# Phi products of two groups in one PSUM bank, and slot sums two at a time

## The chip, the cores and the metric

One core of a Trainium2 chip runs the whole program. The metric is the time of the program on the device in microseconds, the median of several runs. Engines are named as in the profile: PE is TensorE (matmuls), PEld its weight loads, DVE is VectorE, ACT is ScalarE, POOL is GpSimd, SP is SyncE, which sends off the DMAs here.

## The reference, cut to what matters

```python
X = rfft(x, axis=1)                       # x: 8 batches x 2496 x 256
Yr = Xr @ w_r - Xi @ w_i + b_r            # and Yi likewise
Yr = sign(Yr) * max(abs(Yr) - 0.01, 0)    # soft threshold, Yi likewise
y = irfft(Y, n=2496)                      # 19968 tokens of 256
logits = y @ phi                          # 32 slots: 8 experts x 4
d = softmax(logits, axis=0)               # over all tokens
slot_input = d.T @ y                      # 32 x 256
slot_out = relu(slot_input @ w1) @ w2     # per expert
out = softmax(logits, axis=1) @ slot_out
```

## The kernel before

The inverse transform is linear, so the kernel never needs y itself: it multiplies the thresholded spectrum by phi (the **Phi product**), transforms the 32 columns of the result back to logits, and sums the slots on the spectrum's side too.

A batch is done in five **groups** (0 to 4) of four frequency rows; eight batches make 40 **steps**, s = 5b + group. A step runs on PE through `px` (second half of the forward transform, two halves c), `pk` and `py` (the linear layer, `lin_k` and `lin_y`, for two halves e of the 256 features, with c 0 and c 1 summed in turn) and, from `lin_y`, on DVE and POOL to the thresholded spectrum `rt`. Between these stand `pa` matmuls, the first half of the forward transform of a later batch.

`tp_p(s)` takes the spectrum `rt` of a step: 8 matmuls of 32 x 128 onto four strips of a bank `pq` (the Phi product), a copy of 128 x 128 by ACT into `lg`, one transposition of `lg` back into the bank, and a signed copy by DVE into `p_sb`. `tp_t` transposes `rt` itself (`pt`) and copies it to tiles `T` for the slot sums.

When all five groups of a batch are in `p_sb`, `c_stages(b)` runs beside the next batch's five steps: `pg`, a DMA through DRAM (`gd`, `gp`), ACT's `chpL` and DVE's `clpL` (a split into two parts), `pL` (logits), DVE's running maxima `mx`, a transposition `pm`, the batch maximum `mall`, `dg`, `pb`, exponentials `ee`, `pe`, a DMA through DRAM again (`ed`, `eb`), `chpd` and `clpd`, `pd`, and `dd`. Then `slots_acc` adds a group's **slot sum** into the bank `pr`: 4 matmuls of 32 x 256 onto its four strips, one call for each of the five groups; group 0's has 4 more of one column (`zcol`). The trace counts two instructions for each of these matmuls, so a Phi product is x16 and a slot sum x8 there. So a slot sum belongs to a batch two before the one whose Phi product stands beside it.

The order of the instructions is written by hand: every piece of work is a generator that yields the time at which its next part stands in the program, a heap calls the parts in order of these times, and each engine keeps that order. A step is four units of that time. `tp_p(s)` stands at 4s + 6.5 (`LAG` is 6), which is between the two c halves of `py` (e = 1) of the step after. `PLAN["pr"]` holds the times of a batch's five slot sums, in units from 20b + 26; before, each stands directly ahead of a Phi product, except batch 4's first, which stands by itself. Tiles come from rings: the banks `px` and `pa`, `pk` and `py`, `pq` and `pt` have two each, `pr` one; `rt` has a ring of four.

Of the kernel before, what the change touches and what calls it, by code (L numbers as in the profile page):

```python
# [11 lines left out]
F32 = mybir.dt.float32  # L12
# [5 lines left out]
B, N, D = 8, 2496, 256  # L18
# [5 lines left out]
S = 32  # L24
# [28 lines left out]
def _constants():  # L53
# [83 lines left out]
    "pe": [11.35, 12.35],  # L137
    "cm": 14.3,
    "pd": [16.75, 17.5],
    "pr": [20.49, 24.49, 28.49, 32.489999999999995, 36.489999999999995],  # L140
    "au": [[1.4, 3.4, 5.4, 7.4, 9.4, 11.4, 13.4, 15.4, 17.4, 19.4],
           [1.4, 3.4, 5.4, 7.4, 9.4, 10.85, 11.7, 13.4, 15.4, 17.4, 18.85, 19.7]],
    "tho": 1.4,
# [5 lines left out]
    "ao": 0.25,  # L149
    "ko": 0.915,  # L150
    "to": 0.7,
    "late": {'6': {'cms': [11.5, 19.69, 854.1, 854.2, 854.2, 854.2], 'pd': [20.25, 20.62], 'pr': [31.55, 31.6, 31.65, 31.7, 31.75], 'pL': [6.05, 6.5], 'pm': 8.05, 'pb': 9.05, 'eo': 0.4, 'pe': [11.1, 11.5], 'pg': [0.875, 1.275], 'fr': {'sinv': 0, 'm2': 0, 'f1': 0, 'suni': 0}}, '5': {'cms': [14.3, 14.8, 15.6, 20.0, 20.8, 21.5], 'pg': [1.1, 1.8], 'pL': [6.1, 6.8], 'pm': 8.05, 'pb': 9.05, 'fr': {'sinv': 1, 'm2': 1, 'f1': 1, 'suni': 0}, 'pe': [11.35, 12.35], 'pd': [18.9, 19.3], 'pr': [40.2, 40.21, 40.22, 40.23, 40.24]}, '4': {'pr': [18.4, 20.49, 24.49, 28.49, 32.49]}},
    "T_": {'wl': [[-45, 'r'], [-44, 'r'], [-43, 'r'], [-31.0, 't'], [-30.7, 't'], [-29.4, 't'], [-27.6, 't'], [-27.8, 't'], [-11, 'a'], [-10.3, 'a'], [-9.6, 'a'], [-9.45, 'sm'], [-9.4, 'xs'], [-8.3, 'x'], [-8.1, 'x'], [1.06, 'x'], [1.07, 'h'], [1.08, 'h'], [13.55, 'h'], [13.55, 'h'], [13.55, 'h'], [13.55, 'h'], [13.55, 'h'], [13.61, 't'], [13.61, 't'], [13.61, 't'], [13.61, 't'], [13.61, 't'], [13.7, 'T'], [13.7, 'T'], [13.7, 'T']], 'cl': 1.02, 'cp': 46.5, 'ct': 46.6, 'du': [[-4.5, 0], [-2.4, 0], [1.2, 0]], 'd1': [5, 2, 4, 0, 0, 0], 'cm': [19.9, 19.91, 19.92, 25, 25.1, 25.2], 'cm7': [0.1, 0.12, 0.3, 0.4, 1, 1], 'ye': 0.2, 'te': [[5.6, 0.2], [5.5, 0.4]], 'pg': [-7, -3.25, -0.35], 'yt': 0.5, 'wr': -30.6, 'tp': [0, 0.9, 1.05, 0.3], 'tt': [[-3.6, -0.3, -0.25, -0.2, -6.5], [0.6, 0.7, 0, 0, 0], [12, 12.1, 12.2, 12.3, 12.4]], 'tg': {(5, 4): ('ps', 'pl'), (5, 0): ('pl', 'ps')}, 'eg': {(5, 4, 1): 'A', (6, 2, 1): 'A', (6, 4, 0): 'V', (6, 4, 1): 'A'}, 'z': 13.55, 'th': [0.1, 0.12], 'tl': [0.2, 0.25]},
    "f1": [1.5, 2.15],
    "ap1": 1.9,
# [30 lines left out]
def fourier_soft_moe_kernel(ctx: ExitStack, tc: tile.TileContext, t: dict, out: bass.AP):  # L186
# [55 lines left out]
    def mm(**kw):  # L242
        tc.keep_in_program_order(nc.tensor.matmul(**kw))  # L243
# [60 lines left out]
    for z, (n, w) in zip((pk0, pk1), PACK.items()):  # L304
        o = 0
# [243 lines left out]
    def lin_y(s, e):  # L549
        b, grp = steps[s]  # L550
        end = s == ns - 1
        t0 = 4 * s + 1 + (PLAN["T_"]["ye"] if end else 1.35) * e
        yield t0
        py = psum("pl", f"py{b}_{grp}_{e}")
        lin(py, e, 0, xts[(s, 0)], grp == 0)
        if s == 0 and e == 0:
            yield t0 + 0.03
        if e == 1 and not end:
            t0 = 4 * s + 3
            yield t0  # L560
# [13 lines left out]
        if b == B - 3 and grp < KG:
            rt = hd_part(f"rt{b}_", grp, e).rearrange("p (j c q) -> p j c q", j=KG, c=2)
        else:
            rt = wtile([128, KG, 2, 64], F32, "T" if b >= B - 2 else "rt", f"rt{b}_{grp}_{e}")
        yield t0 + (PLAN["T_"]["th"][e] if end else PLAN["tho"])
        L_("th", s, e).tensor_scalar(out=rt, in0=ut, scalar1=LAM, scalar2=-LAM, op0=ALU.min, op1=ALU.max)
        yield t0 + (PLAN["T_"]["tl"][e] if end else PLAN['tlo'])  # L580
        L_("tl", s, e).tensor_tensor(out=rt, in0=ut, in1=rt, op=ALU.subtract)
        tts[(s, e)] = rt

    def tp_p(s):
        b, grp = steps[s]
        n = 4 * s + LAG
        d = PLAN["T_"]["tp"] if s >= ns - 2 else PLAN["tp"]
        yield n + d[0]
        if grp == 0:
            psb[b] = wtile([128, K1, S], F32, "p_sb", f"p_sb{b}")  # L590
        pq = psum("pt", f"pq{b}_{grp}")
        ks = slice(grp * KG, grp * KG + KG)
        rv = [tts[(s, e)].rearrange("p j c q -> p j (c q)") for e in range(2)]
        if s == ns - 1:
            for e in range(2):
                for j in range(KG):
                    mm(
                        out=pq[:, 128 + S * j : 128 + S * j + S],
                        lhsT=rv[e][:, j],
                        rhs=phr[:, e, :],  # L600
                        start=(e == 0 and j == 0),
                        stop=(e == 1),
                        skip_group_check=True,
                    )
        else:
            for e in range(2):
                for j in range(KG):
                    mm(
                        out=pq[S * j : S * j + S, 0:128],
                        lhsT=phr[:, e, :],  # L610
                        rhs=rv[e][:, j],
                        start=(e == 0),
                        stop=(e == 1),
                        skip_group_check=True,
                    )
            yield n + d[1]
            lg = wtile([128, 128], F32, "lg", f"lg{b}_{grp}")
            A.copy(out=lg, in_=pq[:, 0:128])
            yield n + d[2]
            tr(pq[:, 128:256], lg, ident)  # L620
        yield n + d[3]
        V.tensor_tensor(
            out=psb[b][:, ks, :],
            in0=pq[:, 128:256].rearrange("p (j s) -> p j s", s=S),
            in1=sgn[:, ks].unsqueeze(2).broadcast_to([128, KG, S]),
            op=ALU.mult,
        )

    def tr(out, in_, identity):
        tc.keep_in_program_order(nc.tensor.transpose(out=out, in_=in_, identity=identity))  # L630
# [544 lines left out]
    rhs = []  # L1175
# [178 lines left out]
```

## Time and profile before

| | us |
|---|---|
| median of 3 runs | 529.37 (529.04 to 529.81) |
| span of the profiled execution | 528.2 |
| PE busy | 508.5 (96%) |
| DVE busy | 410.7 (78%) |
| ACT busy | 311.1 (59%) |
| POOL busy | 295.0 (56%) |

The granted clock of TensorE is at its full level (2.4 GHz) up to the last of forty slices. Busy time of PE counts overlapping matmuls as one; the chain of waits follows the work that ended last backwards, and its entry for an instruction is the time that passed until the next entry, so a run of matmuls reads shorter there than the sum of their own durations. A timeline row that stands for several instructions has the start of the first. In it an idle time stands in brackets with what ended it.

### The profile page before, as it was taken

How to read it: one execution, taken by the hardware profiler on the slowest of the kernel's cores; microseconds unless marked ns; L12 is line 12 of the kernel's file. 1: busy time of each engine (PE TensorE's matmuls, PEld its weight loads, DVE VectorE, ACT ScalarE, POOL GpSimd, SP SyncE). 2: the span in 40 equal slices, each digit the busy share in tenths (PEclk: the TensorE clock that was granted, in tenths of full speed). 3: DMA queues.
4: the chain of work that ended last, by engine and by line, in shares of the span. 5: the costliest groups of instructions: out<-in, count | busy, mean ns of one | idle time of the engine just before them, and what ended most of it. 6: DMA issues, size and time to landing. Idle time of an engine off the chain costs nothing.

```text
span 528.2 us, 12045 instructions
## 1 busy us (share of the span) xinstructions
PE 508.5 (96%) x4473; PEld 442.1 (84%) x4473; DVE 410.7 (78%) x802; ACT 311.1 (59%) x679; POOL 295.0 (56%) x279
## 2 busy tenths in 40 slices
PE   8999999999999999999999999999999999999991
PEld 8888899998898989898989898888998887458880
DVE  3876886799978998899789989887898856256671
ACT  2666666768666866686668665645434346138771
POOL 0567587768675766676667666856575403053310
PEclk9999999999999999999999999999999999999996
DMA  8545456674765565556655665686665477979998
GB/s 296 185 165 186 159 182 224 169 236 125 269 171 177 153 224 157 194 157 217 172 182 149 228 185 199 161 302 181 234 166 158 159 173 210 403 245 397 402 407 338
DMA packets 90002, 114.85 MB, mean 217 GB/s; under 512 B 46462, under 2 KB 65852, under 8 KB 89944
## 3 DMA queue, kind: packets, MB, share of 16 engines
q1 hardware_dynamic: 89233, 112.90, 65.3%
q10 hardware_dynamic: 711, 1.19, 0.7%
q8 instruction: 35, 0.57, 0.4%
q14 instruction: 23, 0.19, 0.1%
HBM read 66.72 MB, written 47.34 MB: 216 GB/s over the span
## 4 chain that ended last, share of the span: by engine, by line
PE 78%; DVE 9%; DMA 4%; ACT 3%; issue 2%; POOL 1%; SPq 1%; ACTq 0%; DVEq 0%; POOLq 0%
PE py L243 19%; PE px L243 12%; PE pq L243 9%; PE pa L243 8%; PE pk L243 8%; PE pt L630 6%; PE pr L243 4%; PE pc L1153 2%; PE pe L243 2%; PE pg L243 2%; PE pL L243 1%; PE po L243 1%; DVE ut L182 1%; PE hps L243 1%; DVE xtl L182 1%
## 5 line engine op out<-in xcount | busy, mean ns | idle before, releaser
L182 POOL TENSOR_TENSOR rt<-ut,rt 128x512 f32<-128x512 f32 x79 | 108.0, 1366 | 21.6 <-DVE rt L182 20.7
L182 POOL TENSOR_TENSOR xs<-xsm,xs 128x256 fp32r<-128x256 f32 x78 | 58.5, 750 | 101.5 <-DVE xs L182 74.1
L182 POOL TENSOR_TENSOR xl<-xr,xh 117x512 fp32r<-117x512 f32 x72 | 99.1, 1377 | 11.5 <-ACT xh L182 11.5
L243 PEld LDWEIGHTS px<-smov,ap 128*128 128x128 f32 x640 | 79.7, 191 | 9.4 <-issue 3.1
L243 PE MATMUL px<-smov,ap 128*128 128x128 f32 x640 | 85.6, 277 | 2.0 <-ACT ast L182 0.8
L182 ACT CAST xth<-px 128x512 fp32r<-128x512 f32 x80 | 47.0, 588 | 55.8 <-PE py L243 33.9
L182 DVE SCALAR_TENSOR_TENSOR ut<-py,pk,k 128x256 f32<-128x256 f32 x160 | 69.5, 476 | 10.7 <-PE py L243 10.2
L182 ACT COPY ast<-pa 128x512 f32<-128x512 f32 x75 | 44.3, 591 | 46.7 <-PE pa L243 46.6
L182 DVE TENSOR_TENSOR xtl<-px,xth 128x512 fp32r<-128x512 f32 x80 | 54.6, 683 | 16.3 <-ACT xsm L182 15.8
L243 PE MATMUL pk<-xs,w_rh 128*128 128x256 f32 (+1 forms) x320 | 66.0, 290 | 0.3 <-POOL xs L182 0.3
L182 DVE TENSOR_SCALAR rt<-ut 128x512 f32<-128x512 f32 x69 | 56.9, 824 | 0.5
L243 PE MATMUL py<-xth,nwsh 128*128 128x256 f32 (+1 forms) x160 | 53.3, 333 | 0.4 <-DVE ut L182 0.2
L243 PEld LDWEIGHTS pk<-xs,w_rh 128*128 128x128 f32 x320 | 51.8, 189 | 1.1 <-POOL xs L182 0.5
L182 ACT CAST xh<-xr 117x512 fp32r<-117x512 f32 x75 | 47.3, 634 | 0.0
L630 PE MATMUL pt<-pk,rt 128*128 128x128 f32 x320 | 45.4, 274 | 0.2
L182 ACT COPY T<-pt 128x512 f32<-128x512 f32 x67 | 39.7, 600 | 8.9 <-PE pt L630 7.5
L243 PE MATMUL py<-xth,wdh 128*128 128x256 f32 (+1 forms) x160 | 44.8, 280 | 0.0
L243 PE MATMUL py<-xtl,nwsh 128*128 128x256 f32 (+1 forms) x160 | 44.5, 278 | 0.0
L243 PE MATMUL py<-xtl,wdh 128*128 128x256 f32 (+1 forms) x160 | 44.5, 278 | 0.0
L243 PE MATMUL py<-xth,wdl 128*128 128x256 f32 (+1 forms) x160 | 44.4, 278 | 0.0
L243 PE MATMUL py<-xth,nwsl 128*128 128x256 f32 (+1 forms) x160 | 44.4, 278 | 0.0
L243 PE MATMUL pk<-xs,w_rl 128*128 128x256 f32 (+1 forms) x160 | 44.4, 277 | 0.0
(195 smaller groups left out, 1200.7 us busy)
## 6 DMA issues: line engine op xcount, KB each, us to landing
out<-ost SPq DMA_DIRECT2D x37, 512.0 KB
xr<-in_x SPq DMA_DIRECT2D x35, 512.0 KB
ap<-adr SPq DMA_DIRECT2D x70, 256.0 KB
adr<-ast SPq DMA_DIRECT2D x21, 768.0 KB
w<-in_moe_w SPq DMA_DIRECT2D x25, 512.0 KB
w<-in_moe_w SPq DMA_DIRECT2D x12, 256.0 KB
x<-in_x SPq DMA_DIRECT2D x11, 256.0 KB
eb<-ed SPq DMA_DIRECT2D x16, 160.0 KB
```

What stands on the lines that cost most here:

```text
L182: return lambda *a, **k: self.tc.keep_in_program_order(f(*a, **k))
L243: tc.keep_in_program_order(nc.tensor.matmul(**kw))
L630: tc.keep_in_program_order(nc.tensor.transpose(out=out, in_=in_, identity=identity))
L1153: nc.tensor.transpose(out=pc[:, i * P1 : (i + 1) * P1], in_=chls[b][x][:, 2 * (r + i) : 2 * (r + i) + 2].rearrange("p g h s -> p (g h s)") ...
```

## The change

Steps in `PAIRED` (groups 1 and 3 of the batches 0 to 6 without step 1, and group 1 of the last batch; 14 steps) no longer have a `tp_p` of their own. The `tp_p` of the step behind takes both: 16 matmuls into 256 columns of one bank, one copy of 128 x 256, two transpositions, one signed copy of 128 x 256. The slot sums of groups 1 and 3 move to the places of groups 0 and 2; of batch 4 the first two stand at the place of group 0 and the other three at that of group 2. Up to batch 4 the `rt` of the first step of a pair lies in a tile `rtx` in a room that batch 0 used and then left, two such tiles in turn, instead of in the ring of four. No matmul is added or taken away, and the transpositions `pt` stay where they were.

```diff
@@ -37,6 +37,7 @@
 XTRA = {2: (2, 5), 3: (5, 8)}
+PAIRED = {NGRP * b + g for b in range(B - 1) for g in (1, 3)} - {1} | {NGRP * (B - 1) + 1}
 
 
 def _tokens():
@@ -137,7 +138,7 @@
     "pd": [16.75, 17.5],
-    "pr": [20.49, 24.49, 28.49, 32.489999999999995, 36.489999999999995],
+    "pr": [20.49, 20.495, 28.49, 28.495, 36.49],
@@ -149,7 +150,7 @@
-    ... '4': {'pr': [18.4, 20.49, 24.49, 28.49, 32.49]}},
+    ... '4': {'pr': [20.49, 20.495, 28.49, 28.495, 28.497]}},
@@ -573,6 +574,10 @@
             )
         if b == B - 3 and grp < KG:
             rt = hd_part(f"rt{b}_", grp, e).rearrange("p (j c q) -> p j c q", j=KG, c=2)
+        elif s in PAIRED and b < B - 3:
+            if e == 0:
+                rtx[s] = hd_tile((len(rtx) + 1) % 2, f"rtx{s}")
+            rt = rtx[s][:, 512 * e : 512 * e + 512].rearrange("p (j c q) -> p j c q", j=KG, c=2)
         else:
             rt = wtile([128, KG, 2, 64], F32, "T" if b >= B - 2 else "rt", f"rt{b}_{grp}_{e}")
         yield t0 + (PLAN["T_"]["th"][e] if end else PLAN["tho"])
@@ -581,17 +586,20 @@
         L_("tl", s, e).tensor_tensor(out=rt, in0=ut, in1=rt, op=ALU.subtract)
         tts[(s, e)] = rt
 
-    def tp_p(s):
+    def tp_p(*group):
+        s = group[-1]
         b, grp = steps[s]
         n = 4 * s + LAG
+        m = len(group)
         d = PLAN["T_"]["tp"] if s >= ns - 2 else PLAN["tp"]
         yield n + d[0]
         if grp == 0:
             psb[b] = wtile([128, K1, S], F32, "p_sb", f"p_sb{b}")
         pq = psum("pt", f"pq{b}_{grp}")
-        ks = slice(grp * KG, grp * KG + KG)
-        rv = [tts[(s, e)].rearrange("p j c q -> p j (c q)") for e in range(2)]
+        ks = slice((grp - m + 1) * KG, grp * KG + KG)
         if s == ns - 1:
+            o = 128
+            rv = [tts[(s, e)].rearrange("p j c q -> p j (c q)") for e in range(2)]
             for e in range(2):
                 for j in range(KG):
                     mm(
@@ -603,26 +611,30 @@
                         skip_group_check=True,
                     )
         else:
-            for e in range(2):
-                for j in range(KG):
-                    mm(
-                        out=pq[S * j : S * j + S, 0:128],
-                        lhsT=phr[:, e, :],
-                        rhs=rv[e][:, j],
-                        start=(e == 0),
-                        stop=(e == 1),
-                        skip_group_check=True,
-                    )
+            o = 128 * m
+            for i, u in enumerate(group):
+                rv = [tts[(u, e)].rearrange("p j c q -> p j (c q)") for e in range(2)]
+                for e in range(2):
+                    for j in range(KG):
+                        mm(
+                            out=pq[S * j : S * j + S, 128 * i : 128 * i + 128],
+                            lhsT=phr[:, e, :],
+                            rhs=rv[e][:, j],
+                            start=(e == 0),
+                            stop=(e == 1),
+                            skip_group_check=True,
+                        )
             yield n + d[1]
-            lg = wtile([128, 128], F32, "lg", f"lg{b}_{grp}")
-            A.copy(out=lg, in_=pq[:, 0:128])
+            lg = wtile([128, 256], F32, "lg", f"lg{b}_{grp}")
+            A.copy(out=lg[:, :o], in_=pq[:, :o])
             yield n + d[2]
-            tr(pq[:, 128:256], lg, ident)
+            for i in range(m):
+                tr(pq[:, o + 128 * i : o + 128 * i + 128], lg[:, 128 * i : 128 * i + 128], ident)
         yield n + d[3]
         V.tensor_tensor(
             out=psb[b][:, ks, :],
-            in0=pq[:, 128:256].rearrange("p (j s) -> p j s", s=S),
-            in1=sgn[:, ks].unsqueeze(2).broadcast_to([128, KG, S]),
+            in0=pq[:, o : o + 128 * m].rearrange("p (j s) -> p j s", s=S),
+            in1=sgn[:, ks].unsqueeze(2).broadcast_to([128, m * KG, S]),
             op=ALU.mult,
         )
 
@@ -886,6 +898,7 @@
     for g in range(0, G, GP):
         step_to(a_unit(1, g))
     steps = [(b, g) for b in range(B) for g in range(NGRP)]
+    rtx = {}
     ns = len(steps)
     TB = 4 * ns + LAG
     xts, tts, psb, tls, kss = {}, {}, {}, {}, {}
@@ -977,7 +990,8 @@
         step_to(lin_k(s_))
         for e in range(2):
             step_to(lin_y(s_, e))
-        step_to(tp_p(s_))
+        if s_ not in PAIRED:
+            step_to(tp_p(s_ - 1, s_) if s_ - 1 in PAIRED else tp_p(s_))
         for h in range(2):
             b_, g_ = steps[s_]
             key = (g_, h) if b_ == B - 2 and g_ >= 2 else (7, 0) if (b_, g_, h) == (B - 1, 0, 0) else None
```

On PE, group 1 of batch 3 (`pr1` is the slot sum of batch 1, `pq3` the Phi product of batch 3, `py3_2_1` the linear layer of its group 2, e = 1). Before:

```order
L243 MATMUL py3_2_1_3056<-xtl3_2_0_2826,wdh_247 128x256
L243 MATMUL pr1_2901<-T1_1_0_1533,dd1_2620 32x256 x2
L243 MATMUL pr1_2901<-T1_1_1_1560,dd1_2620 32x256 x2
L243 MATMUL pq3_1_3073<-rt3_1_0_2878,pk0_117 32x128 x4
L243 MATMUL pq3_1_3073<-rt3_1_1_2942,pk0_117 32x128 x4
L243 MATMUL py3_2_1_3056<-xth3_2_1_2896,nwsh_244 128x256
L243 MATMUL py3_2_1_3056<-xth3_2_1_2896,nwsl_245 128x256
```

and now:

```order
L244 MATMUL py3_2_1_3034<-xth3_2_0_2800,wdh_247 128x256
L244 MATMUL py3_2_1_3034<-xth3_2_0_2800,wdl_248 128x256
L244 MATMUL py3_2_1_3034<-xtl3_2_0_2801,wdh_247 128x256
L244 MATMUL py3_2_1_3034<-xth3_2_1_2871,nwsh_244 128x256
L244 MATMUL py3_2_1_3034<-xth3_2_1_2871,nwsl_245 128x256
L244 MATMUL py3_2_1_3034<-xtl3_2_1_2872,nwsh_244 128x256
```

The slot sum and the Phi product are gone from between the two halves of py.

On PE, group 2 of batch 3, ahead of `pm2`, the transposition of batch 2's maxima. Before:

```order
L243 MATMUL py3_3_1_3215<-xtl3_3_0_2988,wdh_247 128x256
L243 MATMUL pr1_2901<-T1_2_0_1691,dd1_2620 32x256 x2
L243 MATMUL pr1_2901<-T1_2_1_1721,dd1_2620 32x256 x2
L243 MATMUL pq3_2_3231<-rt3_2_0_3049,pk0_117 32x128 x4
L243 MATMUL pq3_2_3231<-rt3_2_1_3099,pk0_117 32x128 x4
L755 MATMUL pm2_3240<-pk0_117,mx4_2_3207 128x117
L243 MATMUL py3_3_1_3215<-xth3_3_1_3064,nwsh_244 128x256
```

and now:

```order
L244 MATMUL py3_3_1_3176<-xtl3_3_0_2966,wdh_247 128x256
L244 MATMUL pr1_2876<-T1_2_0_1680,dd1_2588 32x256 x2
L244 MATMUL pr1_2876<-T1_2_1_1710,dd1_2588 32x256 x2
L244 MATMUL pr1_2876<-T1_3_0_1828,dd1_2588 32x256 x2
L244 MATMUL pr1_2876<-T1_3_1_1859,dd1_2588 32x256 x2
L244 MATMUL pq3_2_3196<-rtx16_2853,pk0_117 32x128 x8
L244 MATMUL pq3_2_3196<-rt3_2_0_3027,pk0_117 32x128 x4
L244 MATMUL pq3_2_3196<-rt3_2_1_3062,pk0_117 32x128 x4
L767 MATMUL pm2_3213<-pk0_117,mx4_2_3168 128x117
L244 MATMUL py3_3_1_3176<-xth3_3_1_3042,nwsh_244 128x256
```

Two slot sums and two Phi products stand in front of `pm2` in place of one of each.

On PE, group 0 of batch 3, where batch 1's slot sums begin. Before:

```order
L243 MATMUL py3_1_1_2886<-xtl3_1_0_2665,wdh_247 128x256
L243 MATMUL pr1_2901<-T1_0_0_1373,dd1_2620 32x256 x2
L243 MATMUL pr1_2901<-T1_0_1_1404,dd1_2620 32x256 x2
L243 MATMUL pr1_2901<-zcol_121,dd1_2620 32x1 x4
L243 MATMUL pq3_0_2911<-rt3_0_0_2716,pk0_117 32x128 x4
L243 MATMUL pq3_0_2911<-rt3_0_1_2781,pk0_117 32x128 x4
L243 MATMUL py3_1_1_2886<-xth3_1_1_2739,nwsh_244 128x256
```

and now:

```order
L244 MATMUL pr1_2876<-T1_0_0_1367,dd1_2588 32x256 x2
L244 MATMUL pr1_2876<-T1_0_1_1398,dd1_2588 32x256 x2
L244 MATMUL pr1_2876<-zcol_121,dd1_2588 32x1 x4
L244 MATMUL pr1_2876<-T1_1_0_1514,dd1_2588 32x256 x2
L244 MATMUL pr1_2876<-T1_1_1_1541,dd1_2588 32x256 x2
L244 MATMUL pq3_0_2890<-rt3_0_0_2682,pk0_117 32x128 x4
L244 MATMUL pq3_0_2890<-rt3_0_1_2755,pk0_117 32x128 x4
L244 MATMUL py3_1_1_2861<-xth3_1_1_2705,nwsh_244 128x256
```

Group 1's slot sum has come up behind group 0's.

## Rows read from the trace of the kernel before

**Rows 1.** Page, sections 1 and 4: busy time, chain that ended last.

```profile
PE 508.5 (96%) x4473; PEld 442.1 (84%) x4473; DVE 410.7 (78%) x802; ACT 311.1 (59%) x679; POOL 295.0 (56%) x279
...
PE 78%; DVE 9%; DMA 4%; ACT 3%; issue 2%; POOL 1%; SPq 1%; ACTq 0%; DVEq 0%; POOLq 0%
```

**Rows 2.** Stretches: length, busy PE, PEld, DVE, ACT, POOL (x), clock, DMA.

```profile
213.00:266.00 53.00, 52.87 (x496) 47.90 (x494) 47.03 (x91) 35.73 (x78) 34.71 (x31) 1.00 0.60 186
...
318.00:345.00 27.00, 26.45 (x241) 22.69 (x241) 24.07 (x48) 17.26 (x38) 19.38 (x19) 1.00 0.61 183
```

**Rows 3.** Timeline of PE, 207 to 216 us: start, length.

```profile
207.32 0.28 PE L243 MATMUL py<-xtl,wdh 128*128 128x256 f32 x1
207.53 0.64 PE L243 MATMUL pr<-T,dd 128*32 128x256 f32 x8
207.99 0.62 PE L243 MATMUL pq<-rt,pk 128*32 128x128 f32 x16
208.54 0.38 PE L243 MATMUL py<-xth,nwsh 128*128 128x256 f32 x1
208.76 0.28 PE L243 MATMUL py<-xth,nwsl 128*128 128x256 f32 x1
208.88 0.28 PE L243 MATMUL py<-xtl,nwsh 128*128 128x256 f32 x1
...
210.17 0.60 PE L630 MATMUL pt<-pk,rt 128*128 128x128 f32 x4
210.60 1.06 PE L243 MATMUL px<-smov,ap 128*128 128x128 f32 x8
...
215.24 0.32 PE L243 MATMUL pL<-chpL,m2h 120*117 120x352 f32 x1
```

**Rows 4.** Chain of waits, in order of time: start, time until the next entry.

```profile
71.56 0.71 PE py L243 x6
72.27 0.57 PE pq L243 x16
72.84 0.91 PE py L243 x6
...
208.17 0.44 PE pq L243 x16
```

**Rows 5.** Timeline of DVE, 209 to 224 us.

```profile
209.08 0.41 DVE L182 TENSOR_TENSOR xsm<-px,xsm 128x256 f32<-128x256 f32 x1
...
214.52 0.53 DVE L182 TENSOR_REDUCE mx<-pL 117x32 f32<-117x352 f32 x1 [0.30 <-ACT L L182]
...
219.47 0.28 DVE L182 TENSOR_REDUCE mall<-pm 128x1 f32<-128x117 f32 x1 [0.91 <-PE pm L755]
...
223.88 0.28 DVE L182 TENSOR_TENSOR p_sb<-pq,pk 128x128 f32<-128x128 f32 x1
```

**Rows 6.** Groups by form: busy us, mean ns.

```profile
L182 DVE TENSOR_TENSOR xsm<-px,xsm 128x256 f32<-128x256 f32 x80 | 32.9, 412 | 0.0
```

**Rows 7.** Timeline of ACT, pieces between 207 and 342 us.

```profile
207.58 0.59 ACT L182 CAST xth<-px 128x512 fp32r<-128x512 f32 x1 [0.95 <-PE py L243]
...
211.23 0.88 ACT L182 CAST chpL<-gp 120x352 fp32r<-120x352 f32 x2 [0.39 <-DMA gp<-gd]
...
237.96 0.82 ACT L182 CAST chpd<-eb 128x320 fp32r<-128x320 f32 x2
...
341.22 0.82 ACT L182 CAST chpd<-eb 128x320 fp32r<-128x320 f32 x2 [0.37 <-DMA eb<-ed]
```

**Rows 8.** Chain of waits in batch 4's stage, 319 to 352 us.

```profile
319.36 0.74 PE pL L243 x3
...
333.88 2.79 DMA ed<-ea
...
337.33 3.79 DMA eb<-ed
...
351.51 1.13 PE px L243 x8
```

More of the change, by code (lines that the diff above doesn't have):

```diff
@@ L151 @@
     "to": 0.7,
-    "late": {'6': {'cms': [11.5, 19.69, 854.1, 854.2, 854.2, 854.2], 'pd': [20.25, 20.62], 'pr': [31.55, 31.6, 31.65, 31.7, 31.75], 'pL': [6.05, 6.5], 'pm': 8.05, 'pb': 9.05, 'eo': 0.4, 'pe': [11.1, 11.5], 'pg': [0.875, 1.275], 'fr': {'sinv': 0, 'm2': 0, 'f1': 0, 'suni': 0}}, '5': {'cms': [14.3, 14.8, 15.6, 20.0, 20.8, 21.5], 'pg': [1.1, 1.8], 'pL': [6.1, 6.8], 'pm': 8.05, 'pb': 9.05, 'fr': {'sinv': 1, 'm2': 1, 'f1': 1, 'suni': 0}, 'pe': [11.35, 12.35], 'pd': [18.9, 19.3], 'pr': [40.2, 40.21, 40.22, 40.23, 40.24]}, '4': {'pr': [18.4, 20.49, 24.49, 28.49, 32.49]}},
+    "late": {'6': {'cms': [11.5, 19.69, 854.1, 854.2, 854.2, 854.2], 'pd': [20.25, 20.62], 'pr': [31.55, 31.6, 31.65, 31.7, 31.75], 'pL': [6.05, 6.5], 'pm': 8.05, 'pb': 9.05, 'eo': 0.4, 'pe': [11.1, 11.5], 'pg': [0.875, 1.275], 'fr': {'sinv': 0, 'm2': 0, 'f1': 0, 'suni': 0}}, '5': {'cms': [14.3, 14.8, 15.6, 20.0, 20.8, 21.5], 'pg': [1.1, 1.8], 'pL': [6.1, 6.8], 'pm': 8.05, 'pb': 9.05, 'fr': {'sinv': 1, 'm2': 1, 'f1': 1, 'suni': 0}, 'pe': [11.35, 12.35], 'pd': [18.9, 19.3], 'pr': [40.2, 40.21, 40.22, 40.23, 40.24]}, '4': {'pr': [20.49, 20.495, 28.49, 28.495, 28.497]}},
     "T_": {'wl': [[-45, 'r'], [-44, 'r'], [-43, 'r'], [-31.0, 't'], [-30.7, 't'], [-29.4, 't'], [-27.6, 't'], [-27.8, 't'], [-11, 'a'], [-10.3, 'a'], [-9.6, 'a'], [-9.45, 'sm'], [-9.4, 'xs'], [-8.3, 'x'], [-8.1, 'x'], [1.06, 'x'], [1.07, 'h'], [1.08, 'h'], [13.55, 'h'], [13.55, 'h'], [13.55, 'h'], [13.55, 'h'], [13.55, 'h'], [13.61, 't'], [13.61, 't'], [13.61, 't'], [13.61, 't'], [13.61, 't'], [13.7, 'T'], [13.7, 'T'], [13.7, 'T']], 'cl': 1.02, 'cp': 46.5, 'ct': 46.6, 'du': [[-4.5, 0], [-2.4, 0], [1.2, 0]], 'd1': [5, 2, 4, 0, 0, 0], 'cm': [19.9, 19.91, 19.92, 25, 25.1, 25.2], 'cm7': [0.1, 0.12, 0.3, 0.4, 1, 1], 'ye': 0.2, 'te': [[5.6, 0.2], [5.5, 0.4]], 'pg': [-7, -3.25, -0.35], 'yt': 0.5, 'wr': -30.6, 'tp': [0, 0.9, 1.05, 0.3], 'tt': [[-3.6, -0.3, -0.25, -0.2, -6.5], [0.6, 0.7, 0, 0, 0], [12, 12.1, 12.2, 12.3, 12.4]], 'tg': {(5, 4): ('ps', 'pl'), (5, 0): ('pl', 'ps')}, 'eg': {(5, 4, 1): 'A', (6, 2, 1): 'A', (6, 4, 0): 'V', (6, 4, 1): 'A'}, 'z': 13.55, 'th': [0.1, 0.12], 'tl': [0.2, 0.25]},
```

## The prediction

> **What bounds the kernel now.** I read the page first, then the busy time by stretches, then the chain and the timelines of the stretches in which the change works. TensorE (PE) is busy 96% of the span and makes up 78% of the chain that ended last, VectorE (DVE) 9% [rows 1]. That says "PE-bound", but the stretches say more. In the steady cycle of five steps from 213 to 266 us PE is busy 52.87 of 53 us, and DVE 47 of the same 53; from 318 to 345 us, where the stage of batch 4 runs, PE leaves 0.55 us of 27 open [rows 2]. So PE sets the pace, DVE has some 6 us of air in 53, and whoever takes work from PE has to ask at each place whether the next matmul's data is there earlier. The profiled execution's span is 528.2 us against a median of 529.4 us; I add differences to the median, since the 1.2 us between them lie around the span and the change doesn't touch them.
>
> **What the change takes from PE.** A Phi product writes 32 columns of the array, its neighbours 128, and going there and back costs time. In the timeline of PE at 207 us [rows 3] matmuls of py follow each other every 0.12 us (208.76, 208.88). From the last py (207.32) to the first pr it is 0.21; the 16 pq from 207.99 to 208.54 take 0.55, where the same 16 hold 0.44 in the chain of waits [rows 4]; the first py behind takes 0.22 (208.54 to 208.76). So a visit costs (0.21 - 0.12) + (0.55 - 0.44) + (0.22 - 0.12) = 0.30 us. A visit of pq alone shows nearly the same: 0.57 for 0.44, and six py behind it 0.91 [rows 4], of which 0.71 is what six py take without a switch [rows 4]: 0.33. The 14 pairs save 14 visits, since the slot sums of groups 1 and 3 move to groups 0 and 2, and batch 4's sums come together and save a fifteenth (it stood alone). Gross: 15 x 0.30 = 4.5 us of PE, no matmul less.
>
> **What it takes from DVE and ACT.** The copy of the logits to lg (ACT) and the signed copy to p_sb (DVE) become one of 256 columns for two of 128. The p_sb of 128 is 0.28 us [rows 5]; 256 columns from PSUM cost 0.41 on DVE in the xsm copies [rows 6]. So 2 x 0.28 - 0.41 = 0.15 us of DVE per pair, 2 us in all. I take nothing for it: at the vacated place the 0.28 falls into DVE's idle time, and at the merged one the copy is 0.13 longer than the one it replaces. The order of SyncE's and GpSimd's instructions is unchanged, so no DMA is queued elsewhere. The spectra that wait go to rooms whose last readers belong to batch 0; I price this at nothing, and nothing there is waited for.
>
> **What the removal is worth where it is made.** In the cycle at 207 us group 1's place loses pr (0.46, 207.53 to 207.99), pq 0.55 and two edges of 0.09 and 0.10, so 1.20 us [rows 3], and a little later one transposition, 0.11 by the four of pt from 210.17 to 210.60 [rows 3]: 1.31 us. Now look at what comes next. px at 210.60 [rows 3] needs the bank that DVE's xsm reads from 209.08 to 209.49 [rows 5]; that chain begins with ACT's xth at 207.58, which waited for the py in front of the removed place [rows 7], so px can move by 1.1 at most. The second pL at 215.24 [rows 3] needs mx, 214.52 + 0.53 [rows 5], which waited 0.30 us for ACT's copy of pL and otherwise has DVE's clpL in front of it; that one hangs on ACT's chpL at 211.23, which idled 0.39 us for the DMA of gp [rows 7]. That DMA was sent off by pg, ahead of the removed place. So mx gains 0.30, pL as much plus its 0.1 of room: of 1.31 us taken from PE, about **0.4** arrive.
>
> **What the addition costs where it is made.** At group 2's place pr (0.46) and pq (0.44) are put in, and that place stands directly in front of pm, the transposition on which DVE's mall waits (219.47, 0.91 us idle for it) [rows 5]. pm comes 0.90 - 0.4 = 0.5 later. From there DVE works without a hole of note up to its p_sb at 223.88 [rows 5], for which pt waits, and now with 0.13 more: PE is 0.5 to 0.65 late there. The stage's DMAs (ed, eb) pass this on to chpd at 237.96; but chpd there came without idle time behind another copy of ACT's, not behind a wait for the DMA [rows 7], so I let the 0.5 be taken up there. What group 3's place sheds, PE waits off again at the px and pt behind chpd, since DVE is packed from there to the end of the stage, now with a p_sb 0.13 longer: the stage ends about 0.1 late. Behind it group 0's place, in a stretch where PE waits for nothing, gets one pr of 0.46 more. Sum of this cycle: 0.1 + 0.46 = **+0.6 us**. The best it could do is -0.6 (both visits saved), the worst +1.0 (the DMAs pass all of 0.5 on). Three such cycles (batches 1 to 3): I take +0.35 each, under the worked one since it is a tight one, so **+1.0**.
>
> **Batch 4's stage** has no such room [rows 8]. Group 0's pr in front of pg (+0.46) goes into the DMAs to chpL and on over clpL and mx to pL at 319.36, which PE awaits already: group 1's removal at 312 us only makes that wait longer. Then pr and pq, 0.90, in front of pm: +1.36 at mall. The DMAs ed (2.79 us) and eb (3.79) follow, chpd idles for eb here (341.22, 0.37) [rows 7], and DVE goes on from it without a hole to the copy for which px at 351.51 waits [rows 8]. With p_sb's 0.13 and a little more behind it: **+1.6** by 351.5 us.
>
> **The rest.** Batch 0's stage with the pairs from step 3 to 9 has no slot sums; what moves in front of pm and behind is pq and a transposition, 0.44 + 0.12 for each of three pairs; between -0.3 and +0.56 a pair I take +0.3, nearer to the worked cycle: **+1.0**. At 353 us the place of group 0 keeps its visit and gets 0.5 of batch 4's sums; then two sums and a product, 1.37, stand in front of batch 5's pb: bounds -0.6 and +1.9, I take **+1.0**. The last pairs, without slot sums, gain **-0.2**; from 425 us on the kernel waits for outputs, and what came late stays late. Sum: 1.0 + 1.0 + 1.6 + 1.0 - 0.2 = +4.4, so 533.8 us. Several terms are the tight one of a pair of bounds and any unseen room takes from them, so I forecast **533.0 us**, with 530.5 to 535.5 as this case's own range.
>
> **Rivals.** (1) *PE paces everywhere.* The waits that I see close up are fractions of a microsecond, and DVE, eased by 2 us, may draw its chains forward with PE. Then all visits saved arrive: 529.4 - 4.5 = **524.9**. For it speaks PE's 52.87 of 53 us; against it, the px, pL and pt that stand 0.1 to 0.3 us behind their releasers. The Trainium skill (TensorEngine Tiling (Array Packing), Tiling Modes, Key Properties) says that changing the tiling mode drains the engine while changing the tile within a mode doesn't. The 0.30 us of the timeline agree with the first half, and by that rule alone the change would be a gain. (2) *Half and half.* The steady cycles keep their savings (-0.6 each, with batch 0 and the end about -3), batch 4's and 5's stages give +2.6 back: **about 529**, no difference to be measured. (3) *The slow stages take everything.* All three regular cycles at their +1.0 and batch 5 at +1.9 instead of +1.0: 533.8 + 1.95 + 0.9 = **536.6**. Decisive is whether pm's lateness gets through ed and eb to chpd; it does from 0.5 us on.
>
> **How the numbers follow.** Slower by the worked sum 0.50, (1) with its neighbourhood up to 528.3 0.32, (2) 0.12, (3) 0.06. A measurement tells 0.2%, about 1.1 us, from no change: slower 0.56, same 0.12, faster 0.32. The range of 8 in 10 reaches from 525.0 (nearly all of rival 1's saving, leaving out what lies at its end) to 535.5, which leaves out rival 3.
>
> **What would show it.** Right: in the changed trace PE's busy time falls by about 4 us but waits appear in front of px and pL behind the vacated places of groups 1 and 3; DVE's idle time in front of mall grows; chpd in the batch-4 stage comes over 1 us later, counted from the same work. The group-2 visit shows 16 pr, 32 pq in one go with one pair of edges. Wrong: if px and pL follow each other as closely as before and the span of a steady cycle falls under 52.9 us, then the chains moved forward with PE and rival 1 holds; if pt and px behind group 2's place don't wait although pm is late, DVE had room that I didn't see.

## The result, and the profile after

The changed kernel takes **536.13 us** (median of 4 runs, 535.44 to 536.22) against 529.29 us (4 runs): 1.0119 times as long, interval 1.0106 to 1.0131: 6.3 us by the ratio, 6.8 between the medians. The way was forecast, the size wasn't: 533.0 was forecast, with 525.0 to 535.5 as the range, and the time lies 0.6 us above it. Rival 3, "the slow stages take everything", had put 536.6 on it and got a chance of 0.06.

The page of the changed kernel, sections 1 and 4:

```profile
span 534.3 us, 12021 instructions
...
PE 506.3 (95%) x4473; PEld 442.0 (83%) x4473; DVE 411.9 (77%) x788; ACT 310.2 (58%) x665; POOL 296.2 (55%) x279
...
PE 64%; DVE 13%; DMA 10%; ACT 5%; issue 3%; SPq 2%; POOL 1%; ACTq 0%; DVEq 0%; POOLq 0%
```

PE's busy time fell by 2.2 us, not by the 4 that I named, and its share of the chain that ended last fell from 78% to 64%, while DVE's rose from 9 to 13% and the DMAs' from 4 to 10% [rows 1]. So the kernel that PE paced is now paced by others for longer. Three stretches (length, then busy time of PE, PEld, DVE, ACT, POOL): the five steps that answer to the first of [rows 2], batch 4's stage, and what follows it, where batch 5's begins:

```profile
214.50:268.40 53.90, 52.41 (x491) 47.44 (x489) 46.30 (x90) 36.10 (x78) 33.87 (x31) 1.00 0.62 184
...
321.50:349.80 28.30, 26.64 (x258) 23.15 (x257) 24.46 (x47) 17.23 (x38) 20.14 (x19) 1.00 0.60 181
349.80:376.00 26.20, 23.80 (x207) 21.41 (x206) 20.57 (x43) 12.77 (x28) 16.87 (x16) 1.00 0.73 236
```

The last of them in the trace of before:

```profile
345.00:371.00 26.00, 25.42 (x234) 22.34 (x233) 20.62 (x44) 13.00 (x29) 16.89 (x16) 1.00 0.74 235
```

PE stands open for 1.49 us in a steady cycle where it was 0.13, for 1.66 us in batch 4's stage where it was 0.55, and for 2.40 us behind it where it was 0.58.

The visits do what they should. Group 2's, in the timeline of PE (start, length, instruction):

```profile
219.78 0.28 PE L244 MATMUL py<-xtl,wdh 128*128 128x256 f32 x1
219.99 1.07 PE L244 MATMUL pr<-T,dd 128*32 128x256 f32 x16
220.87 0.62 PE L244 MATMUL pq<-rtx,pk 128*32 128x128 f32 x16
221.31 0.62 PE L244 MATMUL pq<-rt,pk 128*32 128x128 f32 x16
221.86 0.32 PE L767 MATMUL pm<-pk,mx 117*128 117x117 f32 x1
```

Two slot sums (219.99 to 220.87) and two products (220.87 to 221.86) share one entry of 0.21 us and one slow last product, as one of each did in [rows 3]. What comes in front of them is the news. Group 1's place and the pL behind it:

```profile
209.11 0.28 PE L244 MATMUL py<-xtl,wdh 128*128 128x256 f32 x1
209.23 0.28 PE L244 MATMUL py<-xth,nwsh 128*128 128x256 f32 x1
...
210.62 0.60 PE L642 MATMUL pt<-pk,rtx 128*128 128x128 f32 x4
211.49 1.13 PE L244 MATMUL px<-smov,ap 128*128 128x128 f32 x8 [0.28 <-ACT ast L183]
...
214.46 0.33 PE L244 MATMUL pL<-chpL,m2l 120*117 120x352 f32 x1
215.44 0.42 PE L244 MATMUL pL<-clpL,m2h 120*117 120x352 f32 x1 [0.65 <-DVE clpL L183]
```

The two halves of py now follow each other at 0.12 us (209.11, 209.23), the visit is gone. But px at 211.49 waits, and the last third of pL at 215.44 waits 0.65 us for DVE's clpL; in [rows 3] nothing stood still in this stretch. The reason is in ACT's timeline, first row, and DVE's, the others (idle time and its end in brackets):

```profile
213.43 0.87 ACT L183 CAST chpL<-gp 120x352 fp32r<-120x352 f32 x2 [2.03 <-DMA gp<-gd]
...
240.74 0.82 ACT L183 CAST chpd<-eb 128x320 fp32r<-128x320 f32 x2 [1.00 <-DMA eb<-ed]
```

```profile
213.95 1.87 DVE L183 TENSOR_TENSOR clpL<-gp,chpL 120x352 fp32r<-120x352 f32 x2 [1.55 <-ACT chpL L183]
...
222.22 0.28 DVE L183 TENSOR_REDUCE mall<-pm 128x1 f32<-128x117 f32 x1 [1.77 <-PE pm L767]
...
226.64 0.41 DVE L183 TENSOR_TENSOR p_sb<-pq,pk 128x256 f32<-128x256 f32 x1
...
238.97 0.41 DVE L183 TENSOR_TENSOR xsm<-px,xsm 128x256 f32<-128x256 f32 x1
```

chpL waits 2.03 us for gp's DMA where it was 0.39 [rows 7]; mall waits 1.77 us for pm where it was 0.91 [rows 5]; and chpd at 240.74 waits 1.00 us for eb's DMA where it did not wait at all [rows 7]. Last, the second px behind group 3's place:

```profile
238.66 0.40 PE L244 MATMUL pa<-xh,f1l 117*128 117x512 f32 x1
239.52 1.13 PE L244 MATMUL px<-smov,ap 128*128 128x128 f32 x8 [0.47 <-DVE xsm L183]
```

It waits for DVE's xsm of 238.97: 0.47 us idle, and 0.63 later than the 0.23 us at which it followed pa before. In the trace of before, the same px followed the pa in front of it at once:

```profile
237.04 0.40 PE L243 MATMUL pa<-xh,f1l 117*128 117x512 f32 x1
237.27 1.06 PE L243 MATMUL px<-smov,ap 128*128 128x128 f32 x8
```

**Where the 6 us arise.** To see it I subtract the start of every px in the trace of before from that in the changed one; the difference is PE's lateness there. Its growth, stage by stage, against the terms of the forecast:

| stretch | forecast | growth seen, us |
|---|---|---|
| start, and batch 0's stage | +1.0 | +0.95 |
| batches 1, 2, 3 | +1.0 | +0.65, +1.43, +0.82 = +2.9 |
| batch 4's stage | +1.6 | +1.3 |
| 353 us, batch 5's stage | +1.0 | +1.8 |
| last pairs, end | -0.2 | -0.75 |

The growth sums to 6.2 us, counted from the first px, which stood 0.26 us earlier than before; the span grew by about 6. The stages of batches 1 to 3, called the regular ones from here on, and batch 5's carry the miss.

### The profile page after: what moved, and what is told of

It reads as the page before. It is cut to its first block, busy times and chain, and to the rows that moved or that the text cites. A ratio compares the mean times of both kernels' runs of the same rounds, so it can differ in the third digit from the quotient of the medians.

```text
span 534.3 us, 12021 instructions
## 1 busy us (share of the span) xinstructions
PE 506.3 (95%) x4473; PEld 442.0 (83%) x4473; DVE 411.9 (77%) x788; ACT 310.2 (58%) x665; POOL 296.2 (55%) x279
## 4 chain that ended last, share of the span: by engine, by line
PE 64%; DVE 13%; DMA 10%; ACT 5%; issue 3%; SPq 2%; POOL 1%; ACTq 0%; DVEq 0%; POOLq 0%
PE py L244 14%; PE px L244 10%; PE pq L244 9%; PE pa L244 6%; PE pk L244 5%; PE pt L642 4%; PE pr L244 4%; DMA gp<-gd 3%; DMA gd<-g_sb 2%; DVE cb L183 2%; DVE xtl L183 2%; SPq L238 2%; PE pL L244 2%; DVE ut L183 2%; PE pd L244 2%
## 5 line engine op out<-in xcount | busy, mean ns | idle before, releaser
L183 POOL TENSOR_TENSOR rt<-ut,rt 128x512 f32<-128x512 f32 x61 | 84.6, 1387 | 18.9 <-DVE rt L183 18.9
L244 PE MATMUL py<-xth,nwsh 128*128 128x256 f32 (+1 forms) x160 | 51.9, 324 | 0.1
L244 PE MATMUL pq<-rhs,ct 128*128 128x512 f32 x156 | 41.4, 405 | 0.3 <-ACT rhs L183 0.3
L183 DVE TENSOR_SCALAR rt<-ut 128x512 f32<-128x512 f32 x51 | 38.7, 760 | 0.5
```

The costliest lines, as they stand in the source:

```text
L183: return lambda *a, **k: self.tc.keep_in_program_order(f(*a, **k))
```

## The experiments

Theory A: places matter. The stage of a batch is one chain (pg, DMA, pL, pm, DVE, pe, DMA, pd, dd), and work in front of pg or pm is paid for, while what group 1's and 3's places shed doesn't come back. Theory B: the paired bank itself costs the time, its one copy behind 32 products. The medians of before lie between 529.3 and 530.0 us, by chip, so runs are compared by their ratio to it.

**One half of the change at a time.** The slot sums alone:

```diff
-    "pr": [20.49, 24.49, 28.49, 32.489999999999995, 36.489999999999995],
+    "pr": [20.49, 20.495, 28.49, 28.495, 36.49],
```

> The kernel before with the slot sums alone moved (groups 1 and 3 to the places of groups 0 and 2, batch 4's as in the change); every group keeps its own Phi product and its own visit to the 32-column strips. Theory A (the stage's chain pg, DMA, pL, pm, DVE, pe, DMA, pd sets the end; work put in front of pg or pm counts in full, work taken from the places of groups 1 and 3 comes back as nothing): 0.46 us more in front of pg and 0.46 in front of pm in each of the five stages with sums, 4.6 us in all, so 533 to 534.5 us. Theory B (the paired bank costs the time: one copy of 256 columns that waits for all 32 products, the longer p_sb behind it): no pair here, the sums only change places, 529.3 us, or less by the one visit that batch 4's lone sum saves.

Measured 532.53 us, ratio 1.0068 (1.005 to 1.0087). And the pairs alone, the changed kernel with the old "pr" list:

> The changed kernel with the slot sums back at their five old places; Phi products and their copies paired as in the change. Theory A: in front of pm stands 0.44 us more and behind it a p_sb that is 0.13 longer, 0.57 in six stages, 3.4 us, less about 1.2 us that the pairs save at the start and at the end, where no such chain runs: 531 to 532 us. Theory B: the whole loss, 535 to 536 us.

Measured 532.04 us, 1.0055 (1.004 to 1.0069). The pairs lie on the upper edge of theory A's range, the sums half a microsecond under theirs. Theory B falls as the sole cause: sums without any pair cost 3 us. But by the px starts the three regular stages cost the sums alone 0.35 us and the pairs alone 0.07, while both together cost 2.9 there; so "comes back as nothing" was wrong too, and that both numbers came near theory A's is luck: it spread the loss evenly over five or six stages, while the pairs lose next to nothing in the regular three, but 0.8 us in batch 0's stage, 0.4 in batch 4's and 1.1 in batch 5's. Where the sums lose theirs is only in part shown: 0.75 us in batch 4's stage, but the profiled execution took 535.5 us against a median of 532.5, and 3.3 us of its loss lie in batch 5's stage. There PE waits 0.62 and 1.07 us for the parts of pL, and from 371.4 to 374.6 us the granted clock is 0.50 (1.2 GHz). So only the regular stages of sums are read here.

**One pair at a time.**

```diff
-PAIRED = {NGRP * b + g for b in range(B - 1) for g in (1, 3)} - {1} | ...
+PAIRED = {NGRP * b + g for b in range(B - 1) for g in (1,)} - {1} | ...
```

> Only groups 1 and 2 are paired (group 1's slot sum at group 0's place); groups 3 and 4 as before the change. Theory A2 (the two single moves cost 3.0 and 2.5 us and both together 6.8: each vacated place gives back only some 0.5 us, since DVE's copy or the stage's DMA stands that near, and what is vacated beyond it becomes a wait): at group 1's place 1.31 us are vacated, 0.46 stands more in front of pg and 0.57 in front of and behind pm, so 0.5 us in each of five to six stages: 531.5 to 533 us. If every saved visit were worth its 0.30 us and places did not matter: 527 us.

Measured 534.1 us, 1.0081 (1.0064 to 1.0098). The other, with `g in (3,)` and group 1's sum at its old place:

> Only groups 3 and 4 are paired (group 3's slot sum at group 2's place, in front of pm); groups 1 and 2 as before the change. Theory A2: 0.46 us more in front of pm, 0.57 at group 4, 1.31 vacated at group 3, of which the changed trace gave back 0.65: 0.4 us in each of five to six stages, 531 to 532.5 us. If this place had room for all of it (the px behind it stands 1.8 us behind its releaser in the trace of before): 527.5 to 528.5 us.

Measured 531.66 us, 1.0032 (1.0017 to 1.0046). Both lose, so neither is a gain that the other spoils; group 1's is the dearer by far. only_g3 lies in its range, only_g1 1.1 us above it: its regular stages take the 0.5 us each that was expected, but batch 4's takes 0.9, since group 1's place gives nothing back there, and batch 5's, where batch 4's sums are moved as well, 1.5.

Now the **prices of the places**. Growth of PE's lateness in the stage of batch 2 (195 to 248 us in the trace of before), between the px in front of and behind each group's place, from the timelines of PE:

| kernel | group 0 | 1 | 2 | 3 | 4 | sum |
|---|---|---|---|---|---|---|
| changed | +0.46 | +0.09 | +1.02 | -0.65 | +0.52 | +1.43 |
| sums | +0.45 | -0.35 | +0.44 | -0.41 | +0.10 | +0.22 |
| pairs | +0.02 | -0.39 | +0.56 | -0.55 | +0.44 | +0.08 |
| only_g1 | +0.45 | -0.38 | +0.56 | 0.00 | 0.00 | +0.63 |
| only_g3 | +0.02 | 0.00 | +0.43 | -0.65 | +0.53 | +0.33 |
| pair_pr1 | +0.03 | -0.42 | +1.01 | -0.65 | +0.52 | +0.48 |
| pair_nocb | +0.46 | +0.06 | +1.00 | -1.31 | +0.44 | +0.64 |
| only_g3_nocb | +0.02 | 0.00 | +0.43 | -1.31 | +0.70 | -0.16 |
| pair_b4 | +0.45 | -0.37 | +1.01 | -0.65 | +0.53 | +0.96 |

The runs from pair_pr1 on are described further below. What is added at groups 0 and 2 costs what it measures, to 0.03 us. What is taken away comes back up to a lid: about 0.4 us at group 1's place, whether 0.46, 0.56 or 1.31 us were vacated (in the changed kernel nothing here, and 0.65, 0.45 and nothing in the stages of batches 1, 3 and 4), and 0.65 at group 3's. At group 3's place the halves stay under the lid (0.41 of 0.46, 0.55 of 0.55), both together don't. This is theory A2, on which the expectations of only_g1 and only_g3 rested.

How far one execution can be trusted: pair_b4 has the same program on PE as the changed kernel up to the last place in batch 4's stage. Its prices agree to 0.02 us everywhere in this stage but at group 1's place, where it gave back 0.37 and the changed kernel's execution nothing; gp's DMA held chpL up for 1.75 us there against 2.03. So up to 0.46 us at that place differs between executions of one program, and the three regular stages, +2.9 us in the changed kernel's, are +2.5 in pair_b4's.

**pm in front of the visit.** If pm's lateness is what costs, pm should go first. In the changed kernel and in the one before:

```diff
-    "pm": 8.56,
+    "pm": 8.45,
```

> The changed kernel with one number altered: pm stands in front of group 2's visit (slot sums and paired products) instead of behind it, up to batch 4's stage. Theory A: in the changed trace mall waited 1.77 us for pm and mx was ready 1.4 us before pm began; so pm comes up to 1.4 us earlier in five stages. What then binds is PE's own work or pg's place, so not all of it comes back: 529 to 532 us. Theory B: the paired bank still does what it did, 535 to 536.5 us.

> The kernel before with the same one number altered: pm in front of group 2's visit (one slot sum, one product). Theory A in its strong form (the chain through pm sets the end already before the change): mall waited 0.91 us, so up to 0.9 us in each of five stages, 525 to 527 us. In its weak form (before the change the chain lies only just behind PE's own work, whose waits sum to some 3 us between 60 and 425 us): 528 to 529.3 us. Theory B says nothing of it: 529.3 us.

Measured 538.8 us (1.0182, 1.0169 to 1.0195) and 532.07 us (1.005, 1.0038 to 1.0062): both slower, by 0.6% than the changed kernel and 0.5% than the one before, against every expectation. The timeline of PE in old_pm shows why:

```profile
219.36 0.28 PE L243 MATMUL py<-xtl,wdh 128*128 128x256 f32 x1
220.16 0.29 PE L755 MATMUL pm<-pk,mx 117*128 117x117 f32 x1 [0.53 <-DVE mx L182]
220.38 0.64 PE L243 MATMUL pr<-T,dd 128*32 128x256 f32 x8
```

and DVE's there:

```profile
220.49 0.28 DVE L182 TENSOR_REDUCE mall<-pm 128x1 f32<-128x117 f32 x1 [0.48 <-PE pm L755]
```

mx isn't ready: from the last py to pm it is 0.80 us where matmuls of py follow each other at 0.12, so PE loses 0.7 us, 0.53 of them idle. In the kernel before, the visit covered just this wait. Both kernels pay 0.45 to 0.5 us more at group 2's place in every regular stage. I had read DVE's 0.91 us in front of mall as pm's lateness; 0.48 of it is left with pm directly behind mx, so half of it is the way from mx over pm to mall. The third attempt put half a py in front of pm, as cover, and the visit behind it:

> The changed kernel with group 2's visit (two slot sums, two products) moved behind the second half of py, and pm directly in front of it, up to batch 4's stage. Theory A2: py's 0.70 us now cover the wait for mx that stalled PE in the two runs with pm first, and pm comes 1.1 us earlier than in the change while PE does the same work: most of the 1.0 us that each stage lost at this place returns, 531 to 533 us. Theory B (the paired bank itself): 536 us.

Measured 538.9 us, 1.0165 (1.0148 to 1.0182), above both. The order of DVE had moved with it: mall came behind a whole xtl, xsm and xs, and pb waited for it:

```profile
222.20 0.28 PE L767 MATMUL pm<-pk,mx 117*128 117x117 f32 x1
...
226.09 0.39 PE L244 MATMUL pb<-dg,ones 32*117 32x32 f32 x2 [0.84 <-DVE dg L183]
```

This run says nothing on the paired bank, since it brought a wait of its own. The fourth moved group 0's visit behind pg besides:

> As the run before, and group 0's visit (two slot sums, one product) moved behind pg, so that pg and its DMA come 1.4 us earlier and the visit lies in the time of that DMA. Theory A2: group 1's vacated time is then no longer a wait for the DMA, another 0.5 to 1 us in each of five stages: 526 to 529.5 us. If the DMA's wait was not the reason that group 1's place gave nothing back: as the run before.

Measured 540.48 us, 1.0197 (1.0181 to 1.0213). In the stage of batch 2 group 1's place now gave back 0.56 us, where the run before had +0.08, and chpL no longer waited for the DMA there, so the DMA was what held it in that stage. But over the regular stages the mean only went from 0.3 to 0.6 us of 1.31, and batch 4's stage gave back nothing in either run, so the DMA is not all that holds this place. Group 0's place cost 0.81 in place of 0.46, and batch 4's stage cost 2.6. DVE stood 2.66 us in front of ut for a py that the visit had pushed back; PE's own timeline shows no wait above 0.17 us at that place, so the cause of the 0.81 stays open:

```profile
209.19 0.88 DVE L183 SCALAR_TENSOR_TENSOR ut<-py,pk,k 128x256 f32<-128x256 f32 x2 [2.66 <-PE py L244]
```

So of these four changes of order none gained; an order that brings pg forward by a whole visit without a new loss was not found, and whether there is one stays open.

**What the lids are.** At group 3's: from mall to the px at 239.52 DVE has one hole of 0.25 us in 17, so that px can come no earlier than pm's lateness allows, less 0.65. If so, taking work from DVE there must lift the lid, with PE's program unchanged. The combine weights are the softmax of a row; the subtraction of its maximum was left out for the batches 0 to 4 (the result is the same but for rounding), two DVE steps of 0.88 and 1.97 us:

```diff
-        V.tensor_reduce(out=cm, in_=L, axis=AX.X, op=ALU.max)
-        V.tensor_tensor(out=cb, in0=L, in1=cm..., op=ALU.subtract)
-        A.activation(out=cb, in_=cb, func=AF.Exp)
+        A.activation(out=cb, in_=L, func=AF.Exp)      # batches 0 to 4
```

> The changed kernel, with the combine weights of batches 0 to 4 taken as exp of the logits without subtracting each token's maximum first: DVE loses cm (0.88 us) and cb (1.97) between pm and the px at which the changed trace waits 0.65 us for DVE's xsm; PE's program is untouched. Theory A3 (from pm to that px the stage is paced by DVE, so that pm's lateness arrives there and group 3's vacated 1.31 us turn half into a wait): the wait goes, 0.65 us in each of five stages and a little more behind it: 532 to 533.5 us. If PE or the DMAs pace that stretch: 535.5 to 536 us.

> The kernel before with the same two DVE steps left out of batches 0 to 4. Theory A3: before the change PE paces this stretch (the px there stands 0.8 us behind its releaser), so DVE's relief is worth little: 528.3 to 529.5 us, and far less than what it gives the changed kernel. If DVE's load costs both kernels alike: 525.5 to 526.5 us.

Measured 531.76 us (1.0035, 1.0021 to 1.005) and 528.36 us (0.9971, 0.996 to 0.9982). The changed kernel gains 0.84%, the kernel before 0.29%, and the table shows it in the right place: group 3's vacated 1.31 us now come back whole. By the px starts 1.9 us of the gain lie in the regular stages, 1.45 in batch 0's and 0.84 in batch 4's. DVE's timeline there, in pair_nocb:

```profile
232.10 0.69 DVE L183 TENSOR_TENSOR xtl<-px,xth 128x512 fp32r<-128x512 f32 x1 [0.24 <-ACT xsm L183]
...
235.45 0.69 DVE L183 TENSOR_TENSOR xtl<-px,xth 128x512 fp32r<-128x512 f32 x1 [0.75 <-ACT xsm L183]
...
237.79 0.88 DVE L183 SCALAR_TENSOR_TENSOR ut<-py,pk,k 128x256 f32<-128x256 f32 x2 [0.54 <-PE py L244]
```

xtl and ut wait for ACT and PE again, so DVE no longer leads. (The edit also spares ACT's exp its wait for DVE's cb, 0.29 us in the changed kernel; the two effects were not separated.) In the kernel before, the same relief changes no regular stage (0.0 us from batch 1 to 3); its 1.5 us come from the stages of batch 0 and batch 4, 0.8 us each.

At group 1's, the lid should be the stage's DMA, which starts with pg; so group 1's slot sum went back, in front of pg no more, and into that wait:

```diff
-    "pr": [20.49, 20.495, 28.49, 28.495, 36.49],
+    "pr": [20.49, 24.49, 28.49, 28.495, 36.49],
```

> The changed kernel with group 1's slot sum back at its own place, as a visit by itself; batch 4's sums as in the change. Theory A3: 0.46 us less in front of pg; at group 1's place the sum and its switch of 0.3 us lie in the wait for the stage's DMA and cost nothing: 0.46 us in each of five stages, 533.5 to 534.5 us. If work in front of pg does not matter: the extra visit costs 0.3 us in each of five stages, 537 to 538 us.

Measured 535.13 us, 1.0091 (1.0076 to 1.0105), a gain of 0.3% on the change, and 0.6 us above the expected range. In the regular stages the lateness grows by 1.3 us instead of 2.9 (2.5 in pair_b4), as the theory has it; batch 5's stage takes 0.4 of that back (+2.2 for +1.8). Two of the four executions had a mean granted clock of 0.988 and 0.989 and took 535.6 and 535.8 us, the other two 0.993 with 533.8 and 534.7, around the end of the expected range; so the miss goes with the lower clock. Both at once:

> The changed kernel with both: group 1's slot sum back at its place, and the two DVE steps left out of batches 0 to 4. Theory A3: the two causes lie in different stretches of the stage, pg to pL and pm to px, so the gains add: 529.5 to 531.5 us. If both act on one and the same wait: no better than the better of the two.

Measured 530.11 us, 1.0007 (0.9996 to 1.0017). The two gains add (0.28 and 0.84% alone, 1.12% together), so the causes are two.

**The two terms left.** Batch 4's sums back at their old places:

> The changed kernel with batch 4's five slot sums back at their old places, the first again alone; all else as in the change. In the changed trace the stage of batch 5 ends 1.8 us later against before than it began, where 1.0 was forecast. If that is the price of two sums and a product, 1.37 us, that stand in front of pb there: 0.9 us (two sums) less 0.3 for the lone visit come back, 535 to 535.5 us. If it is the paired product alone or the DMA of that stage: 536 to 536.5 us.

Measured 535.15 us, 1.0113 (1.0095 to 1.0131). By the runs that can't be told from the change. By the px starts batch 5's stage grows by 1.1 us and not by 1.8, so moving batch 4's sums costs 0.7 there: 0.49 at group 0's place and 0.95 in front of pb, of which 0.71 come back at group 3's. And the pair of groups 3 and 4 with DVE relieved:

> Groups 3 and 4 paired alone, and the two DVE steps left out of batches 0 to 4. Theory A3: with DVE relieved all of the 1.31 us vacated at group 3's place come back, as in the changed kernel with the same relief; against 0.46 in front of pm and 0.57 at group 4 that is a gain of 0.3 us in each of five stages on top of what the relief gives by itself: 526.5 to 528 us, under both kernels. If a saved visit is worth nothing even then: 528.4 us or more.

Measured 527.82 us, 0.9965 (0.995 to 0.998): faster than the kernel before, like old_nocb, and not to be told from it by the runs. By the px starts its three regular stages shrink by 0.72 us, where old_nocb's stay as they were: a saved visit of 0.30 is worth 0.24 on average once DVE doesn't hold it (0.42, 0.16 and 0.13 in the three).

## Why the prediction was off

**Right.** The merged visit has one pair of edges, as forecast; the fifteenth saved visit, that of batch 4's lone sum, was worth nothing: its place takes +0.11 without it and +0.10 with it (pair_b4). Group 1's place gives back about 0.4 of 1.31 in the stage that was worked out: 0.38 in only_g1, 0.37 in pair_b4, but nothing in the profiled execution of the changed kernel. What is put in front of pg and pm counts in full: +0.46 and +1.02 for the 0.46 and 0.90 + 0.13. In batch 4's stage, forecast at +1.6 and measured at +1.3, the mechanism is right up to mall: +0.46 in front of pg, nothing back at group 1's place, +0.88 in front of pm. Its chain of waits (start, length) runs through the DMA, DVE, the visit and DVE again to a px:

```profile
316.05 3.71 DMA gp<-gd
...
319.91 0.50 ACT chpL L183
...
320.97 1.62 DVE clpL L183
...
323.41 0.74 PE pL L244 x3
...
327.46 0.87 PE pq L244 x32
...
328.62 0.29 DVE mall L183
...
342.14 1.98 DVE cb L183
...
344.72 0.34 DVE xsm L183
...
345.20 1.13 PE px L244 x8
```

Behind mall the chain doesn't run over ed and eb, as the forecast had it, but over DVE; with DVE's two steps left out (pair_nocb) the stage takes +0.5. Batch 0's +1.0 took +0.95. Of the signs named, the waits at px and pL, mall's longer wait and the merged visit are in the trace, and chpd of batch 4's stage comes at 346.31 in place of 341.22, 5.1 us later where the stage began 3.6 late.

**Wrong, first: the regular stages.** The step that failed reads "the stage ends about 0.1 late". It let half a microsecond be taken up at chpd, since ACT was not waiting for the DMA there, and had PE wait off behind chpd whatever group 3's place sheds; the product and the transposition that group 4's place gets have no price in it. Measured, without group 0's sum, the regular stages end 0.5 late on average. It is not chpd that binds first. The px behind group 3's second half hangs on DVE, which works from mall on with one hole of 0.25 us, and it had 0.65 us of room. So group 2's place costs 1.02, of group 3's 1.31 us 0.65 come back, group 4's 0.52 are paid, and the stage ends 0.9 late before group 0's sum is counted, less what group 1 gives back. The prediction had the evidence for it, "DVE works without a hole of note", and didn't follow that hole-less row to the px behind group 3.

**Wrong, second: the choice between bounds.** The worked cycle gave +0.6, and I took 0.35 for each of the three because "it is a tight one". No row stood behind that. The bound of +1.0 was the value: (0.65 + 1.43 + 0.82) / 3 = 0.97, or 0.83 in pair_b4. Shading the sum of 533.8 to 533.0 was the same fault. Rival 3, with a chance of 0.06, came nearest by number, in part by luck: its condition, pm's lateness getting through to chpd, is met, since chpd at 240.74 waits for eb, but PE is not held by that. In pair_nocb chpd waits 0.93 us for eb just so, and group 3's 1.31 us come back whole.

**Wrong, third: batch 5.** Between -0.6 and +1.9 I took +1.0; +1.8 came, of which 1.1 are left with batch 4's sums at their old places (pair_b4). The chain of waits there runs through the DMAs and pL and then the visit:

```profile
366.40 3.95 DMA gp<-gd
...
371.34 2.09 DVE clpL L183 x2
...
373.92 0.74 PE pL L244 x3
...
377.77 1.43 PE pr L244 x24
379.20 0.87 PE pq L244 x32
380.07 0.90 PE py L244 x6
380.98 0.32 PE pb L244 x2
```

24 pr and 32 pq, 2.30 us, stand between pm and pb. By places the stage takes +0.49 at group 0, nothing at group 1, +1.78 in front of pb, -0.94 at group 3 and +0.50 at group 4. The upper bound had 0.5 and 1.37 and nothing back, so that its +1.9 agrees is a cancelling of larger terms; why 1.37 us of work cost 1.78 was not followed.

**Not as forecast, and left there.** PE's busy time fell by 2.2 us and not by 4; why the profile's busy time shows half of the saved switches was not followed. On DVE p_sb fell by the 2 us forecast, but its whole busy time rose by 1.2, since cb and xs took 2.6 and 1.9 us longer; this was not followed either.

## What to carry to other kernels

On an engine that is busy 98% of a stretch or more, work *added* in front of what a chain waits for cost its length in these runs, while work *taken away* came back only up to the room of the next wait; so moving work loses the difference, and two moves that each fit in that room can lose together. Before a move, follow the row of every later instruction on the bounding engine to its releaser, and take as the worth of the vacated place the smallest such room, not the length of the work. Where the releaser belongs to an engine that works without a hole, relief of that engine can be worth more than a new order on the first: here two DVE steps less gave 0.3% before the change and 0.8% after it, and the best order tried on the changed kernel, pair_pr1's, 0.3%.

## What the runs showed that I had not expected

A wait that looks idle in one engine's row can already be paid by another's work: the visit in front of pm filled PE's 0.7 us for mx, and putting pm first cost 0.6% in the changed kernel and 0.5% in the one before. And the prices of the places add up: at groups 0 and 2 the changed kernel pays 0.46 and 1.02 where its halves pay 0.45 + 0.02 and 0.44 + 0.56. Only at the lids they don't, and there lies the whole difference between two halves that cost 0.4 us in three stages and a whole that costs 2.9 (2.5 in pair_b4).
